# First query loads in 2 KB rows, landing times of a trace in the planner, and the tail constant behind unit eight

## The chip, the cores and the metric

The kernel runs on one core of a Trainium2 chip. The core has five engines that take instructions in order: TensorE (PE in the profile; its weight loads stand apart as PEld), VectorE (DVE), ScalarE (ACT), GpSimd (POOL) and SyncE (SP, which only issues DMAs here). Transfers run on 16 DMA engines. The metric is the device time of one execution in microseconds.

## The reference

Two stages. The first is a causal retention over 8 batches of 8 heads, 576 positions and 64 dimensions; the second is a two-layer network with a squared ReLU over all 4608 tokens.

```python
scores = scale * np.matmul(q, k.transpose(0, 1, 3, 2))
gamma = 1.0 - 2.0 ** (-5.0 - np.arange(H, dtype=np.float32))
Dmat = np.where(rel >= 0, gamma[:, None, None] ** rel[None, :, :], 0.0)
x = np.matmul(scores * Dmat, v)          # heads side by side: 4608 x 512
h = x @ w_in                             # 512 x 2048
out = np.maximum(h, 0.0) ** 2 @ w_out    # 2048 x 512
```

## The kernel before

**Units and groups.** A unit is 128 positions of one batch with all heads; there are 36, of which four are "tails" made of the last 64 positions of two batches. Two units form a group, so there are 18 groups. Each group passes through retention (scores, mask, state, output, xT) and then through the network: `ph` = w_in times xT (L876), ReLU (L884) and square (L894 or L896) into gT, and the product with w_out into `po`. Group 0 does that last product directly (L916). Every later group does it by Strassen's scheme with seven half-size products (L973): it needs sums of gT blocks (gS, L946, four a group on DVE) and differences of w_out blocks (wT, L827, four in all, on DVE).

**The first eight units are loaded in pairs.** `add_load_pair` brings 256 positions in one DMA of 512 KB; a partition holds two neighbouring positions, so a row is 512 bytes (L316). `add_unit_pair` casts the two halves to fp16 on DVE, ACT or POOL (kx, qx; L424), scales v (vx, L420), transposes k and q on PE into PSUM (psT, L439) and copies them out (kqT, L450). `add_ret_pair` does the rest: scores psc in two halves e, masked with `mask2` (rx, L490), state sums psS, the state R (L461, L514), outputs psO and xT (L577). Later units load q in four DMAs with 1 KB rows (L298), cast on POOL and are transposed by DMA (L400).

**What sets the order.** No order is written by hand: every step is a task of the class `Schedule` with an engine, a key (lower goes first), a planned duration and dependencies. `emit` runs an event loop over these planned times and writes the instructions in the order in which the tasks started. On the chip every engine then runs its list in that order and waits at each instruction for its own data. So a planned duration changes no work, only the order. DMA landings are planned as tasks of the engine SP: a duration, then `after` until the data count as there, with corrections in `LAG`.

**Start.** SP issues k0, q0, v0, k2, q2, v2 in this order (`FIRST`; 0 and 2 are pairs), then POOL issues the eight weight loads w0 to w7 with a cast to fp16 (L331; w0 to w3 are w_in, w4 to w7 are w_out), the first of them not before v0 has landed. k4 waits on SP until w5 has landed. PE has `WARM` matmuls without use (tile warm, L256) with the lowest priority, which fill its list where nothing else was ready in the plan.

**The tail constant.** `make_tail_pool` (L272, L273) makes iota_pt on POOL; then DVE makes vdl_tail (L182) and ACT vdec_tail (L184), which the v of a tail unit needs. `add_gated` enters it under ("v", 4); such a gate is read only in `add_unit`, which makes it wait for that unit's v cast. Unit 4 goes through `add_unit_pair`.

Of the kernel before, what the change touches and what calls it, by code (L numbers as in the profile page):

```python
# [15 lines left out]
class Schedule:  # L16
# [7 lines left out]
    def add(self, eng, key, dur, fn, deps=(), acq=(), after=None, lag=0.0):  # L24
        t = dict(eng=eng, key=key, dur=dur, fn=fn, acq=acq, n=len(self.tasks), users=[], free=[], lag=lag,
                 left=len(deps), ready=0.0, lat=self.LAT[eng] if after is None else after)
        for d in deps:
            d["users"].append(t)
        self.tasks.append(t)
        return t  # L30
# [11 lines left out]
    def emit(self):  # L42
        ready = {e: [] for e in self.LAT}
        busy = {e: False for e in self.LAT}
        events = []
        order = []
        seq = 0

        def push(at, what, t):
            nonlocal seq  # L50
            seq += 1
            heapq.heappush(events, (at, seq, what, t))
        for t in self.tasks:
            if t["left"] == 0:
                heapq.heappush(ready[t["eng"]], (t["key"], t["n"], t))
        now = 0.0
        while True:
            for e in ready:
                if busy[e]:
                    continue  # L60
                held = []
                while ready[e]:
                    item = heapq.heappop(ready[e])
                    t = item[2]
                    if all(self.count[r] >= t["acq"].count(r) for r in t["acq"]):
                        for r in t["acq"]:
                            self.count[r] -= 1
                        t["start"] = now
                        order.append(t)
                        busy[e] = True  # L70
                        push(now + t["dur"], "end", t)
                        break
                    held.append(item)
                for item in held:
                    heapq.heappush(ready[e], item)
            if not events:
                break
            now = events[0][0]
            while events and events[0][0] <= now + 1e-9:
                _, _, what, t = heapq.heappop(events)  # L80
                if what == "end":
                    busy[t["eng"]] = False
                    for w in t["users"]:

                        push(now + (0.0 if w["eng"] == t["eng"] else t["lat"]), "dep", w)
                    for g in t["free"]:
                        push(now + t["lat"], "free", g)
                elif what == "dep":
                    t["left"] -= 1
                    if t["left"] == 0:  # L90
                        push(now + t["lag"], "go", t)
                elif what == "go":
                    heapq.heappush(ready[t["eng"]], (t["key"], t["n"], t))
                else:
                    t["left"] -= 1
                    if t["left"] == 0:
                        self.count[t["res"]] += 1
        assert len(order) == len(self.tasks)
        for t in order:
            t["fn"]()  # L100
# [3 lines left out]
def kernel(  # L104
# [106 lines left out]
    mask2 = const.tile([P, 2, 2, 64], FP32, name="mask2")  # L211
    nc.gpsimd.memset(mask2, 1.0)
    for c in range(2):
        for e in range(2):
            m = mask2[c * 64:(c + 1) * 64, e]
            nc.gpsimd.affine_select(out=m, in_=m, compare_op=ALU.is_ge, fill=0.0, base=-e, pattern=[[1, 2], [2, 64]],  # L216
                                    channel_multiplier=-2)
# [7 lines left out]
    WARM = 34  # L225
# [4 lines left out]
    BESIDE = 1.1  # L230
# [6 lines left out]
    LAG = {"k4": 0.7, "q4": 0.5}  # L237
# [37 lines left out]
    tail_pool = add_gated("POOL", 4, "v", 2.2, make_tail_pool)  # L275
# [32 lines left out]
    def add_load_pair(name, u):  # L308
        n = "kqv".index(name)

        def fn():
            if name != "q":
                tile_of["stage", u] = stage.tile([P, 2, H, 2 * D], FP32, name="pair", tag="wst")
            x = tile_of[name + "32", u] = tile_of["stage", u][:, n % 2]
            b, c = units[u][1:]
            t = nc.sync.dma_start(out=x, in_=(k, q, v)[n][b, :, c * P:(c + 2) * P, :].rearrange("h (p e) d -> p h (e d)", e=2))  # L316
            if (name, u) == ("k", 4):
                behind(t, tile_of["w", 5])
            tile_of["load", name, u] = t
        loaded[name, u] = loaded[name, u + 1] = dma_task(0, 1.81 if loaded else 2.9, fn, acq=("wst",) if name != "q" else (),  # L320
# [4 lines left out]
    def add_weight(i):  # L325
# [10 lines left out]
        t = add("SP", 0, 2.75, lambda: None, deps=last_load + [issue], after=2.1 + LAG.get(f"w{i}", 0.0))  # L336
# [25 lines left out]
    def half(x):  # L362
        return slice(64 * x, 64 * x + 64)
# [39 lines left out]
    def add_unit_pair(u, base):  # L403
# [4 lines left out]
        for i, name in enumerate("kqv"):  # L408
            xs[name] = []
            for e in range(2):  # L410
                eng = ("DVE" if (e if name == "v" else lead) else "ACT" if name == "k" and u >= 4 or u == 2 and e else
                       "DVE" if name == "q" and u == 2 else "POOL")

                def fc(name=name, e=e, eng=eng):
# [4 lines left out]
                    if name == "v":  # L419
                        (nc.vector if eng == "DVE" else nc.gpsimd).tensor_tensor(  # L420
                            out=t.rearrange("p (h d) -> p h d", d=D), in0=x,
                            in1=vdec[f"pair{e}"].rearrange("p (h o) -> p h o", o=1).to_broadcast([P, H, D]), op=ALU.mult)
                    else:
# [10 lines left out]
        for i, name in enumerate("kq"):  # L434
# [9 lines left out]
            for s in range(2):  # L444
                on_act = i == 0 or s == 0 or u > 0

                def fe(i=i, s=s, on_act=on_act):
                    if i == 0:
                        tile_of["kqT", u + s] = work.tile([P, 2 * NP, P], FP16, name="kqT", tag="kqT", bufs=6)
                    (nc.scalar.copy if on_act else nc.vector.tensor_copy)(  # L450
                        out=tile_of["kqT", u + s][:, i * NP:(i + 1) * NP].rearrange("p x (e t) -> p e x t", e=2),
                        in_=tile_of["psT", u, i][:, :, :, half(s)])
# [15 lines left out]
    def add_ret_pair(g):  # L468
# [7 lines left out]
        for e in range(2):  # L476
# [11 lines left out]
            for a in range(2):  # L488
                def fm(e=e, a=a):
                    nc.vector.tensor_tensor(  # L490
                        out=rT[e][:, a], in0=rT["ps", e][a].rearrange("p (n i) -> p n i", i=P),
                        in1=mask2[:, e].rearrange("p (o e) i -> p o (e i)", o=1).to_broadcast([P, NP, P]), op=ALU.mult)
# [80 lines left out]
        for s in range(2):  # L573
            def fx(s=s):
                if s == 0:
                    tile_of["x", g] = x_pool.tile([P, NP, 2 * P], FP16, name="xT", tag="xT")
                nc.vector.tensor_tensor(  # L577
                    out=tile_of["x", g][:, :, s * P:(s + 1) * P].rearrange("p n (i e) -> p n e i", e=2),
                    in0=tile_of["psO", g][s].rearrange("p (n e i) -> p n e i", n=NP, e=2),
                    in1=gam_f.rearrange("p n (i e) -> p n e i", e=2), op=ALU.mult)  # L580
# [120 lines left out]
    def after_sums(g, t, key, res):  # L701
# [24 lines left out]
        r2 = add("DVE", key + 0.3, 0.65, fr2, deps=[r1], acq=("R",))  # L726
# [95 lines left out]
    def add_wT(i, in0, in1):  # L822
        ts = []
        for h in range(2):
# [3 lines left out]
            ts.append(add("DVE", WT_KEY + i, 0.7, f, deps=sum((wcast[j] for j in range(4, 8 if i else 6)), [])))  # L828
# [6 lines left out]
    for x, y in ((t2, t1), (t4, t2)):  # L835
        for p in y:
            for w in x:
                sched.need(w, p)
# [19 lines left out]
    def add_ff(g):  # L858
# [10 lines left out]
        for fb in range(NF // nf):  # L869
# [18 lines left out]
            def fg(fb=fb, on_act=on_act):  # L888
# [6 lines left out]
                else:  # L895
                    nc.vector.tensor_tensor(out=t, in0=rl, in1=rl, op=ALU.mult)  # L896
            r = add("ACT", place(4 * fb + 4), 0.6, fr, deps=[f1[-1]], acq=("rl",))
            sched.free("ff", [r])
            sq.append(add("ACT" if on_act else "DVE", place(4 * fb + 6), 0.63 if on_act else 0.55, fg, deps=[r] + sq[:1],
                          acq=() if fb else ("g",)))  # L900
# [31 lines left out]
    def add_strassen(g, us, base, sq):  # L932
# [7 lines left out]
        def add_sum(k, key, parts, in0, in1, op, deps, start=()):  # L940
            out_ = []
            for h in range(parts):
# [4 lines left out]
                out_.append(add("DVE", key + h, (BESIDE if h else 0.5) if parts > 1 else 0.8, f, deps=deps(h, parts) + list(start)))  # L947
# [164 lines left out]
```

## Time and profile before

| | us |
|---|---|
| median of 8 runs (lowest, highest) | 289.8 (289.52, 290.01) |
| the profiled execution | 289.78 |
| its span, first to last instruction | 288.1 |
| busy: DVE, ACT, POOL | 176.2, 187.4, 85.8 |
| xT of the first group done on DVE | 16.0 |
| first `ph` matmul | 17.73 |
| last matmul ends | 283.96 |
| k0, v0 landed (issue at 0.81 and 1.95; 4.2 and 6.7 us to landing) | 5.0, 8.7 |
| w0, w1 landed (issue at 8.96 and 11.01; 8.4 and 8.8 us to landing) | 17.4, 19.8 |

The profiled execution took 1.68 us more than its span; that share lies before the first and after the last instruction. Times in the text are from the start of the span. The granted clock was 0.998 of full speed. In the profile a busy share is given in tenths for forty slices of the span, a group of instructions by its line in the code and the names of its tiles, and a wait by what released it.

### The profile page before, as it was taken

To read this page: it belongs to the slowest core of one execution; us is meant where nothing else is said; L and a number is where in the kernel's file an instruction comes from. 1 tells how busy PE (TensorE), PEld (TensorE's weight loads), DVE (VectorE), ACT (ScalarE), POOL (GpSimd) and SP (SyncE) were. 2 spreads that over 40 slices of the span, in tenths; PEclk is the share of its full clock that TensorE was granted. 3 is DMA by queue.
4 is the path that set the end of the run, shared out by engine and by line. 5 is a ranking of instruction groups with operands and counts; after the bars stand their busy time and mean duration, and the time that the engine had idled before them with its cause. 6 is when DMAs were issued, how large, how long until landed. Compare 5 with 4: busy or idle time off the path is not lost.

```text
span 288.1 us, 10135 instructions
## 1 busy us (share of the span) xinstructions
PE 281.4 (98%) x4346; PEld 236.4 (82%) x4346; DVE 176.2 (61%) x341; ACT 187.4 (65%) x363; POOL 85.8 (30%) x124
## 2 busy tenths in 40 slices
PE   7999999999999999999999999999999999999994
PEld 3568767888888888888888888888888888888883
DVE  3772389768666756647656575766575566364632
ACT  4558975667585857657576748575848675847830
POOL 5560045333514242433425151534324000000000
PEclk9999999999999999999999999999999999999999
DMA  7999999999999898999789998979889420102004
GB/s 200 276 208 206 247 288 275 180 240 157 237 189 164 211 196 222 173 212 173 202 163 215 219 186 190 203 196 243 182 176 222 106 77 2 73 2 75 0 4 144
DMA packets 122156, 49.94 MB, mean 173 GB/s; under 512 B 94720, under 2 KB 117760, under 8 KB 122112
## 3 DMA queue, kind: packets, MB, share of 16 engines
q1 hardware_dynamic: 117568, 44.84, 70.3%
q0 software_dynamic: 4224, 4.19, 8.8%
q8 instruction: 34, 0.56, 0.9%
q10 hardware_dynamic: 320, 0.26, 0.4%
q14 instruction: 10, 0.08, 0.1%
HBM read 36.70 MB, written 9.44 MB: 160 GB/s over the span
## 4 chain that ended last, share of the span: by engine, by line
PE 91%; DMA 3%; POOL 2%; issue 2%; DVE 0%; POOLq 0%; DVEq 0%
PE ph L876 44%; PE po L973 37%; PE psO L357 4%; DMA w_in<-in_moe_w_in_dram 3%; PE po L916 2%; PE psc L357 2%; PE psS L357 2%; PE psT L439 1%; POOL mask L216 0%; POOL vx L420 0%; POOL w_in L331 0%; DVE o L996 0%; POOL mask_full L208 0%; POOL mask_tail L208 0%; DVE p L1025 0%
## 5 line engine op out<-in xcount | busy, mean ns | idle before, releaser
L876 PE MATMUL ph<-xT,w_in 128*128 128x256 f16 x1152 | 136.6, 273 | 0.2 <-DMA w_in<-in_moe_w_in_dram 0.2
L876 PEld LDWEIGHTS <-w_in 128*128 128x128 f16 x1152 | 111.3, 98 | 14.7 <-DMA w_in<-in_moe_w_in_dram 0.5
L884 ACT ACTIVATE rl<-ph 128x512 f16<-128x512 f32 x144 | 84.3, 586 | 50.6 <-PE ph L876 48.0
L894 ACT ACTIVATE gT<-rl 128x512 f16<-128x512 f16 x118 | 74.4, 631 | 3.4
L973 PEld LDWEIGHTS <-gS 128*128 128x128 f16 x544 | 51.7, 98 | 6.5
L973 PE MATMUL po<-wT,gS 128*128 128x256 f16 x408 | 55.8, 273 | 0.0
L946 DVE TENSOR_TENSOR gS<-gT,gS 128x512 f16<-128x512 f16 (+1 forms) x51 | 30.7, 601 | 23.9 <-ACT gT L894 23.3
L973 PEld LDWEIGHTS <-gT 128*128 128x128 f16 x408 | 39.6, 98 | 4.8
L973 PE MATMUL po<-w_out,gT 128*128 128x256 f16 x272 | 36.7, 273 | 0.0
L387 POOL TENSOR_TENSOR v<-v,vdec_full 128x512 f16<-128x512 f32 x24 | 26.6, 1106 | 26.3 <-DMA v<-in_v_dram 20.8
L946 DVE TENSOR_TENSOR gS<-gT 128x1024 f16<-128x1024 f16 x34 | 25.4, 747 | 7.0 <-ACT gT L894 6.9
L371 POOL CAST kq<-k 128x512 f16<-128x512 f32 x28 | 19.0, 677 | 34.5 <-DMA k<-in_k_dram 31.3
L382 POOL CAST kq<-q 128x512 f16<-128x512 f32 x24 | 15.1, 628 | 36.3 <-DMA q<-in_q_dram 36.2
L896 DVE TENSOR_TENSOR gT<-rl 128x512 f16<-128x512 f16 x26 | 12.2, 467 | 19.7 <-ACT rl L884 19.7
L996 DVE TENSOR_TENSOR o<-po,u 128x256 f32<-128x256 f32 x33 | 13.9, 421 | 15.5 <-PE po L973 7.9
L986 ACT COPY u<-po 128x256 f32<-128x256 f32 x34 | 12.5, 368 | 15.7 <-PE po L973 15.5
L751 DVE TENSOR_TENSOR xT<-psO,gam_full 128x512 f16<-128x512 f32 x28 | 18.0, 684 | 4.4 <-PE psO L357 4.0
L996 DVE TENSOR_TENSOR o<-po,p 128x256 f32<-128x256 f32 x18 | 7.6, 423 | 21.1 <-ACT u L986 13.1
L973 PE MATMUL po<-w_out,gS 128*128 128x256 f16 x136 | 18.0, 273 | 0.0
L973 PE MATMUL po<-wT,gT 128*128 128x256 f16 x136 | 17.6, 273 | 0.0
L692 DVE TENSOR_TENSOR rT<-psc,mask_full 128x512 f16<-128x512 f32 x24 | 15.6, 682 | 3.2 <-PE psc L357 3.0
L1047 ACT COPY o<-po 128x256 f32<-128x256 f32 x16 | 5.9, 370 | 10.4 <-PE po L973 8.8
(82 smaller groups left out, 226.6 us busy)
## 6 DMA issues: line engine op xcount, KB each, us to landing
out_dram<-o SPq DMA_DIRECT2D x32, 256.0 KB, 2.7
k<-in_k_dram SPq DMA_DIRECT2D x24, 256.0 KB, 4.5
q<-in_q_dram SPq DMA_DIRECT2D x96, 64.0 KB, 3.2
v<-in_v_dram SPq DMA_DIRECT2D x24, 256.0 KB, 3.8
pair<-in_k_dram SPq DMA_DIRECT2D x4, 512.0 KB, 7.0
pair<-in_q_dram SPq DMA_DIRECT2D x4, 512.0 KB, 7.0
pair<-in_v_dram SPq DMA_DIRECT2D x4, 512.0 KB, 7.0
w_in<-in_moe_w_in_dram POOLq DMA_DIRECT2D x4, 512.0 KB, 9.1
```

The source lines that it names most:

```text
L357: t = nc.tensor.matmul(out_, lhsT=lhsT, rhs=rhs, start=start, stop=True, skip_group_check=True, tile_position=(64 * row, 64 * col))
L371: op(out=out_.rearrange("p (n b a d) -> p n b a d", n=2, b=2, a=2), in_=in_.rearrange("p (a n b) d -> p n b a d", n=2, a=2))
L382: nc.gpsimd.tensor_copy(out=tile_of["kq", u][:, 1].rearrange("p (t a d) -> p a t d", t=4, a=2), in_=tile_of["q32", u].rearrange("p (a t) d ...
L387: nc.gpsimd.tensor_tensor(out=t, in0=tile_of["v32", u], in1=vdec[kind].rearrange("p (h o) -> p h o", o=1).to_broadcast([P, H, D]), op=ALU. ...
L692: tile_of["masking", g] = nc.vector.tensor_tensor(out=tile_of["rT", g][:, :, a], in0=tile_of["psc", g][a].rearrange("p (s n i) -> p s n i" ...
L751: nc.vector.tensor_tensor(out=tile_of["x", g].rearrange("p n (s e i) -> p e (n s) i", s=n, e=2)[:, c], in0=y.rearrange("p (o t r) -> p o r ...
L876: nc.tensor.matmul(tile_of["ph", g, fb][:, j, :], lhsT=w_in16[:, m, fi * P:(fi + 1) * P], rhs=tile_of["x", g][:, m, :], start=(m == 0), st ...
L884: nc.scalar.activation(out=t, in_=tile_of["ph", g, fb], func=ACTF.Relu)
L894: nc.scalar.activation(out=t, in_=rl, func=ACTF.Square)
L946: nc.vector.tensor_tensor(out=tile_of["S", g][:, k, sl], in0=in0(sl), in1=in1(sl), op=op)
L973: nc.tensor.matmul(tile_of["pb", g, bank], lhsT=left(i), rhs=right[:, i, :], start=(start and i == 0), stop=(i == HF - 1), skip_group_chec ...
L996: nc.vector.tensor_tensor(out=o_tile(u)[:, half * HM:(half + 1) * HM], in0=bank(x), in1=tile_of[name, g], op=ALU.add)
```

## The change

It has four parts.

1. A paired q is loaded by two DMAs of 256 KB, one for each half of the heads; a partition takes eight neighbouring positions of one head in each, a row of 2 KB. Which position lies in which partition and column thereby changes for q, and with it the cast of q, the copy of its transpose (kqT, both for q alone), `mask2` and the order in which xT is written.
2. The planner gets other numbers: planned durations and landings of the loads, a smaller `WARM`, and a model in which certain DVE tasks (`soft`) advance at 0.22 of their speed while a POOL task longer than 0.5 us runs. For group 1 the squares on DVE, the last ReLU and the sums get an earlier key (`HURRY`). A difference of w_out waits only for the weight loads that it reads.
3. All four casts of k and q for units 2 and 3 go to ACT (before: one each on POOL and DVE, two on ACT).
4. The tail constant is entered under ("v", 8), and unit 8 goes through `add_unit`.

```diff
@@ -21,8 +21,10 @@
-    def add(self, eng, key, dur, fn, deps=(), acq=(), after=None, lag=0.0):
-        t = dict(eng=eng, key=key, dur=dur, fn=fn, acq=acq, n=len(self.tasks), users=[], free=[], lag=lag,
+    SHARED = 0.22
+    def add(self, eng, key, dur, fn, deps=(), acq=(), after=None, lag=0.0, soft=False):
+        t = dict(soft=soft, eng=eng, key=key, dur=dur, fn=fn, acq=acq, n=len(self.tasks), users=[], free=[], lag=lag,
                  left=len(deps), ready=0.0, lat=self.LAT[eng] if after is None else after)
@@ -54,6 +56,17 @@
         now = 0.0
+        port = dict(task=None, left=0.0, at=0.0, beside=False)
+        def shared(beside):
+            t = port["task"]
+            if t is not None:
+                port["left"] -= (now - port["at"]) * (self.SHARED if port["beside"] else 1.0)
+                port["at"] = now
+                t["end"] = now + max(port["left"], 0.0) / (self.SHARED if beside else 1.0)
+                push(t["end"], "end", t)
+            port["beside"] = beside
         while True:
@@ -68,7 +81,14 @@
                         busy[e] = True
-                        push(now + t["dur"], "end", t)
+                        t["end"] = now + t["dur"]
+                        if t["soft"]:
+                            port.update(task=t, left=t["dur"], at=now)
+                            shared(port["beside"])
+                        else:
+                            push(t["end"], "end", t)
+                        if e == "POOL" and t["dur"] > 0.5:
+                            shared(True)
                         break
@@ -79,7 +99,14 @@
                 if what == "end":
+                    if abs(t["end"] - now) > 1e-6:
+                        continue
+                    t["end"] = -1.0
                     busy[t["eng"]] = False
+                    if t["soft"]:
+                        port["task"] = None
+                    elif t["eng"] == "POOL" and t["dur"] > 0.5:
+                        shared(False)
                     for w in t["users"]:
@@ -208,12 +235,12 @@
-    mask2 = const.tile([P, 2, 2, 64], FP32, name="mask2")
+    mask2 = const.tile([P, 2, 8, 16], FP32, name="mask2")
     nc.gpsimd.memset(mask2, 1.0)
             m = mask2[c * 64:(c + 1) * 64, e]
-            nc.gpsimd.affine_select(out=m, in_=m, compare_op=ALU.is_ge, fill=0.0, base=-e, pattern=[[1, 2], [2, 64]],
+            nc.gpsimd.affine_select(out=m, in_=m, compare_op=ALU.is_ge, fill=0.0, base=-e, pattern=[[1, 8], [8, 16]],
                                     channel_multiplier=-2)
@@ -222,19 +249,19 @@
     L = 2 * NF
-    WARM = 34
+    WARM = 26
     EARLY = 20
     QL = 0.8
-    BESIDE = 1.1
+    HURRY = 60
     PAUSE = 1.5
     JOIN = 5
-    LAG = {"k4": 0.7, "q4": 0.5}
+    LAG = {"k0": 0.3, "q0": 0.6, "v0": 0.3, "k2": 0.2, "q2": 0.5, "v2": 1.0, "w2": 0.7, "w7": 1.4, "k4": 0.3, "q4": 1.1, "v4": 0.9, "q6": 0.8, "v6": 0.2}
     LAG_T, LAG_O = 1.5, 5.0
@@ -272,7 +299,7 @@
-    tail_pool = add_gated("POOL", 4, "v", 2.2, make_tail_pool)
+    tail_pool = add_gated("POOL", 8, "v", 0.45, make_tail_pool)
     tail_dec = add("DVE", 0, 0.3, lambda: make_vdec("tail", tile_of["iota_pt"]), deps=[tail_pool])
@@ -313,11 +340,17 @@
             b, c = units[u][1:]
-            t = nc.sync.dma_start(out=x, in_=(k, q, v)[n][b, :, c * P:(c + 2) * P, :].rearrange("h (p e) d -> p h (e d)", e=2))
+            src = (k, q, v)[n][b, :, c * P:(c + 2) * P, :]
+            if name == "q":
+                for a in range(2):
+                    t = nc.sync.dma_start(out=x[:, NP * a:NP * a + NP].rearrange("p t d -> p (t d)"),
+                                          in_=src.rearrange("(a x) (r t) d -> a r x (t d)", a=2, t=8)[a])
+            else:
+                t = nc.sync.dma_start(out=x, in_=src.rearrange("h (p e) d -> p h (e d)", e=2))
             if (name, u) == ("k", 4):
             tile_of["load", name, u] = t
-        loaded[name, u] = loaded[name, u + 1] = dma_task(0, 1.81 if loaded else 2.9, fn, acq=("wst",) if name != "q" else (),
+        loaded[name, u] = loaded[name, u + 1] = dma_task(0, 2.9 if not loaded else 1.41 if name == "q" else 1.81, fn, acq=("wst",) if name != "q" else (),
                                                          after=2.1 + LAG.get(name + str(u), 0.0))
@@ -333,7 +366,7 @@
         issues.append(issue)
-        t = add("SP", 0, 2.75, lambda: None, deps=last_load + [issue], after=2.1 + LAG.get(f"w{i}", 0.0))
+        t = add("SP", 0, 2.58, lambda: None, deps=last_load + [issue], after=3.0 + LAG.get(f"w{i}", 0.0))
         last_load[:] = [t]
@@ -408,8 +441,7 @@
             for e in range(2):
-                eng = ("DVE" if (e if name == "v" else lead) else "ACT" if name == "k" and u >= 4 or u == 2 and e else
-                       "DVE" if name == "q" and u == 2 else "POOL")
+                eng = ("DVE" if (e if name == "v" else lead) else "ACT" if name == "k" and u >= 4 or u == 2 and name != "v" else "POOL")
@@ -420,6 +452,9 @@
                             in1=vdec[f"pair{e}"].rearrange("p (h o) -> p h o", o=1).to_broadcast([P, H, D]), op=ALU.mult)
+                    elif name == "q":
+                        x = tile_of["q32", u].rearrange("p (a t) (s d) -> p a (t s) d", a=2, s=2)[:, :, NP * e:NP * e + NP]
+                        engines[eng](out=t.rearrange("p (t a d) -> p a t d", t=NP, a=2), in_=x)
                     else:
@@ -447,9 +482,13 @@
                         tile_of["kqT", u + s] = work.tile([P, 2 * NP, P], FP16, name="kqT", tag="kqT", bufs=6)
-                    (nc.scalar.copy if on_act else nc.vector.tensor_copy)(
-                        out=tile_of["kqT", u + s][:, i * NP:(i + 1) * NP].rearrange("p x (e t) -> p e x t", e=2),
-                        in_=tile_of["psT", u, i][:, :, :, half(s)])
+                    out_, in_ = tile_of["kqT", u + s][:, i * NP:(i + 1) * NP], tile_of["psT", u, i]
+                    if i == 0:
+                        out_, in_ = out_.rearrange("p x (e t) -> p e x t", e=2), in_[:, :, :, half(s)]
+                    else:
+                        out_ = out_.rearrange("p x (t r) -> p t x r", r=16)
+                        in_ = in_.rearrange("p e y (r x) -> p (e y) x r", x=NP)[:, :, :, 16 * s:16 * s + 16]
+                    (nc.scalar.copy if on_act else nc.vector.tensor_copy)(out=out_, in_=in_)
                 es.append(add("ACT" if on_act else "DVE", base + 3 + i + s / 2, 0.66, fe, deps=[t] + T["kqT", u + s],
@@ -489,7 +528,7 @@
                         out=rT[e][:, a], in0=rT["ps", e][a].rearrange("p (n i) -> p n i", i=P),
-                        in1=mask2[:, e].rearrange("p (o e) i -> p o (e i)", o=1).to_broadcast([P, NP, P]), op=ALU.mult)
+                        in1=mask2[:, e].rearrange("p (o t) r -> p o (t r)", o=1).to_broadcast([P, NP, P]), op=ALU.mult)
                 ms.append(add("DVE", base + 5 + e, 0.66, fm, deps=[t] + ms))
@@ -575,9 +614,9 @@
                 nc.vector.tensor_tensor(
-                    out=tile_of["x", g][:, :, s * P:(s + 1) * P].rearrange("p n (i e) -> p n e i", e=2),
-                    in0=tile_of["psO", g][s].rearrange("p (n e i) -> p n e i", n=NP, e=2),
-                    in1=gam_f.rearrange("p n (i e) -> p n e i", e=2), op=ALU.mult)
+                    out=tile_of["x", g][:, :, s * P:(s + 1) * P].rearrange("p n (r t) -> p n r t", t=8),
+                    in0=tile_of["psO", g][s].rearrange("p (n t r) -> p n r t", n=NP, t=8),
+                    in1=gam_f.rearrange("p n (r t) -> p n r t", t=8), op=ALU.mult)
             T["x", u + s] = add("DVE", base + 25 + s, 0.7, fx, deps=[t] + ([T["x", u]] if s else []), acq=() if s else ("x",))
@@ -723,7 +762,7 @@
         r1 = add("DVE", key + 0.2 - URGENT, 0.69, fr1, deps=[r0])
-        r2 = add("DVE", key + 0.3, 0.65, fr2, deps=[r1], acq=("R",))
+        r2 = add("DVE", key + 0.3, 0.62, fr2, deps=[r1], acq=("R",), soft=True)
         T["Rm", g], T["R", g], T["Rread", g], T["Rmread", g] = r0, r2, [], r1
@@ -825,7 +864,7 @@
                 nc.vector.tensor_tensor(out=wT[i][:, sl], in0=in0[:, sl], in1=in1[:, sl], op=ALU.subtract)
-            ts.append(add("DVE", WT_KEY + i, 0.7, f, deps=sum((wcast[j] for j in range(4, 8 if i else 6)), [])))
+            ts.append(add("DVE", WT_KEY + i, 0.68, f, deps=wcast[4 + h] + (wcast[6 + h] if i else []), soft=True))
         return ts
@@ -833,9 +872,8 @@
     for x, y in ((t2, t1), (t4, t2)):
-        for p in y:
-            for w in x:
-                sched.need(w, p)
+        for w, p in zip(x, y):
+            sched.need(w, p)
     wT_done = {7: t3, 6: t2, 5: t1, 4: t4}
@@ -894,10 +932,10 @@
                     nc.vector.tensor_tensor(out=t, in0=rl, in1=rl, op=ALU.mult)
-            r = add("ACT", place(4 * fb + 4), 0.6, fr, deps=[f1[-1]], acq=("rl",))
+            r = add("ACT", place(4 * fb + 4) - HURRY * (g == 1 and fb == 7), 0.6, fr, deps=[f1[-1]], acq=("rl",))
             sched.free("ff", [r])
-            sq.append(add("ACT" if on_act else "DVE", place(4 * fb + 6), 0.63 if on_act else 0.55, fg, deps=[r] + sq[:1],
-                          acq=() if fb else ("g",)))
+            sq.append(add("ACT" if on_act else "DVE", place(4 * fb + 6) - HURRY * (g == 1 and not on_act), 0.63 if on_act else 0.43, fg, deps=[r] + sq[:1],
+                          acq=() if fb else ("g",), soft=not on_act))
             sched.free("rl", [sq[-1]])
@@ -944,7 +982,7 @@
                     nc.vector.tensor_tensor(out=tile_of["S", g][:, k, sl], in0=in0(sl), in1=in1(sl), op=op)
-                out_.append(add("DVE", key + h, (BESIDE if h else 0.5) if parts > 1 else 0.8, f, deps=deps(h, parts) + list(start)))
+                out_.append(add("DVE", key + h - HURRY * (g == 1), 0.43 if parts > 1 else 0.72, f, deps=deps(h, parts) + list(start), soft=True))
             sums[k] = out_
         nb = len(sq) // 2
```

## The prediction

> **What bounds the kernel now.** I read the stretches of the span first, with the busy time of each engine in each (columns: stretch, its length, busy us and instructions of PE, PEld, DVE, ACT, POOL, then clock, DMA share and GB/s), and beside it the same stretches for the useless tile warm.
>
> ```profile
> 0.00:17.00 17.00, 15.11 (x202) 7.58 (x202) 10.70 (x49) 8.58 (x19) 11.21 (x31) 1.00 1.02 233
> 17.00:20.00 3.00, 2.77 (x50) 2.15 (x50) 2.90 (x7) 1.15 (x3) 2.36 (x4) 1.00 1.24 206
> 20.00:52.00 32.00, 31.82 (x450) 24.19 (x449) 19.20 (x33) 24.45 (x47) 8.26 (x10) 1.00 1.15 249
> 52.00:283.00 231.00, 230.72 (x3641) 201.84 (x3640) 142.24 (x252) 153.25 (x296) 63.95 (x80) 1.00 0.74 160
> ```
> ```profile
> 0.00:17.00 17.00, 10.91 (x34) 1.00 1.02 233
> 17.00:20.00 3.00, 0.10 (x1) 1.00 1.24 206
> 20.00:52.00 32.00, 0.00 (x0) 1.00 1.15 249
> ```
>
> From 20 us on PE is idle for 0.18 + 0.28 us in all: nothing is to be won there. In the first 20 us it works 17.88 us, but 11.01 of these are warm matmuls, so only 6.87 us are of use. All that can be gained lies in the first 20 us, and what happens later can only lose. The timeline of PE shows what ends that phase (columns: start, length, instruction, idle time before and its releaser):
>
> ```profile
> 16.06 1.04 PE L256 MATMUL warm<-wT 128*128 128x512 f16 x4
> 17.03 0.77 PE L357 MATMUL psc<-kqT 64*64 64x128 f16 x32
> 17.73 1.92 PE L876 MATMUL ph<-xT,w_in 128*128 128x256 f16 x16
> 19.89 1.48 PE L876 MATMUL ph<-xT,w_in 128*128 128x256 f16 x12 [0.23 <-DMA w_in<-in_moe_w_in_dram]
> 21.30 0.64 PE L357 MATMUL psO<-rx,vx 64*64 64x128 f16 x32
> ```
>
> The last real wait is for w1 at 19.89. The chain of waits, cut to this stretch, leads there as well:
>
> ```profile
> 8.96 0.98 POOL w_in L331
> 9.95 0.07 issue
> 10.02 0.99 POOL vx L420
> 11.01 8.84 DMA w_in<-in_moe_w_in_dram
> 19.84 0.05 issue
> 19.89 1.48 PE ph L876 x12
> ```
>
> Its 8.84 us are not the cost of one transfer but a place in a queue. The DMA view of 2 to 13 us and of 13 to 33 us (packets, mean rate) shows that the engines never pause:
>
> ```profile
> DMA packets 6167, 3.12 MB, mean 284 GB/s; under 512 B 83, under 2 KB 6167, under 8 KB 6167
> ```
> ```profile
> DMA packets 4154, 4.15 MB, mean 207 GB/s; under 512 B 125, under 2 KB 4150, under 8 KB 4150
> ```
>
> First come the six paired loads in 512 B packets, then the weights, whose 207 GB/s written are 414 GB/s read, since the cast halves them. Each load delays all behind it. Issue plus time to landing gives k0 5.0, q0 6.8, v0 8.7, k2 10.5, v2 14.0, w0 17.4, w1 19.8, w2 22.4, w3 24.9 us: a paired load takes 1.8 us of the stream, a weight 2.5.
>
> [...] 1 KB rows of later q loads land 64 KB in 0.16 us (issues at 68.3 and 69.0 landed after 4.1 and 3.6 us, all four within 0.5 us), 1.3 us for 512 KB. [...] The kqT copy on DVE does 128x512 in 424 ns, faster than the 679 ns of a masked 128x512 from fp32 PSUM[...], and the new copy reads with a step of four. [...] gS of 128x1024 took 931 ns at 47.73, beside casts on POOL, against 688 elsewhere.
>
> **The change part by part.**
>
> *q in 2 KB rows.* The same 512 KB per pair in 256 packets instead of 1024. Bounds: 1.27 us at the 414 GB/s at which the weights' 2 KB rows are read[...]. I take 1.34, near the rate seen on this chip[...]: 0.47 us saved a load. q0 and q2 stand ahead of w1, so 2 x 0.47 = **0.94 us**[...]. The second issue costs SP some 0.43 us (the 1 KB-row issues at 69.0 and later). It hides: v0 is issued at 1.95, k2 at 3.36, seconds in the queue before their turn; without that cover v0 would be 0.43 later. w0's own issue waits for v0, which comes 0.47 earlier (q0 alone). Only 7 packets of its queue are seen before 13 us, while the paired packets run until 13.4; they would now end near 12.5 and w0's packets could start from 12.4, so no hole opens. q4 and q6 save 0.94 more behind the weights.
>
> *What is late next.* With w1 at 18.9, ph of w0 must be done by then: w0 at 16.4, 1.75 us of matmul, 18.2. It needs xT of group 0, at 16.0 now. That chain moves too: k0 landed at 5.0, but the timeline of DVE has its cast behind vdl_tail, which waited 2.55 us for iota_pt:
>
> ```profile
> 5.73 0.23 DVE L182 TENSOR_SCALAR vdl_tail<-lnrow,iota_pt 128x8 f32<-128x8 f32 x1 [2.55 <-POOL iota_pt L273]
> 5.86 0.76 DVE L424 CAST kx<-pair 128x512 f16<-128x512 f32 x2
> ```
>
> This wait goes (part 4) and gives some 0.7 us; q0 comes 0.47 earlier. Against it the strided DVE copy of q for unit 1 goes from 0.42 to at most 0.69 (+0.27). So xT falls near 15.5, before 16.4: all three are hidden by w0, and cost or give nothing. Without that cover the copy would cost its 0.27. The ACT copies (592 ns) may stay[...]; the trace has none like it. I take 0, since ACT has 1.6 of 4 us free in 12 to 16 us.
>
> *Casts of units 2 and 3.* POOL and DVE lose one of 0.62 and 0.42; ACT gains 2 x 0.62. q2's first cast now stands at 13.48 on DVE, behind the state updates, though q2 is there by about 12.3; on ACT it can go at landing. That takes a us or more off psc of group 1, now at 17.03 just behind the four warm ones. If rx and thus psO of group 1 (1.0 us of PE, now at 21.3, behind w1) come before w1's arrival, PE does up to 0.7 us of it in the gap that opens between 18.2 and 18.9. DVE is the limit: 3.82 and 3.68 of 4 us busy in 12 to 20, with rx ending at 20.0. I expect it to end near 18.7 and count **0.2 us** (0 to 0.7).
>
> *Planner.* 26 instead of 34 warm matmuls: eight of 0.216 are 1.7 us, about what the shorter start takes from the need for them; they never stood before anything that w1 doesn't gate. If too few, PE idles a us; [...] no idle gap in this trace after 1.3 us reaches even 0.3 us. `HURRY` brings four sums and the DVE squares of group 1 ahead of group 2's retention on DVE: of these only the 0.93 us at 47.73 stood behind rx of group 2. xT of group 2 is ready at 50.53 and its ph starts at 51.98, so 1.45 us are free, and group 2's loads come 0.94 to 1.4 earlier. Nothing.
>
> *Same cost.* The mask, xT and q's POOL casts keep sizes and counts; xT of the later units already reads with a step of 16 elements and takes 684 ns against 726 here. The tail constant later costs 0.18 + 0.22 on POOL, 0.23 on DVE and 0.30 on ACT, beside PE.
>
> Sum: 289.78 - 0.94 - 0.2 = **288.6 us**. This is against the profiled execution, 0.02 below the median of 289.8.
>
> **The rivals.** *A, the forecast:* w1 and all behind it move up. [...] *B, more:* psO of group 1 is wholly done before w1; for it, 2 us less on the cast path; against it, the full DVE. 289.78 - 0.94 - 1.0 = 287.8. *C, hidden anyway:* the order planned anew opens small gaps behind 20 us that eat most of it, say 0.04 us in each of 17 groups, 0.7: 289.5. For it, that PE has no gap to lose there and so every change of order is a risk; against it, that DVE has some 40% free. *D, slower:* vdl_tail now stands on DVE behind unit 8's v cast, and DVE waits there if that cast is planned too early, as it waited 2.55 us at the start. The cast ended at 50.97 in the trace, just where xT of group 2 (49.19 to 50.53), rx of group 3 and the sums are queued. If DVE reaches vdl_tail ahead of xT of group 2 and POOL is no earlier than now, then xT comes at 50.97 + 0.45 + 0.23 + 1.35 = 53.0, against a need at 51.98 - 1.14 = 50.84: 2.2 us lost, 1.0 net, 290.8. It decides against the change once that wait makes xT later than 52.6; v of unit 8 landing 1.9 us earlier (all four q) speaks against it. *E, that part 4 doesn't do what it says:* it does move the constant, since unit 4 never reads a gate; but the wait it ends was hidden by w0, so its worth is nothing and it lies inside A, without a chance of its own.
>
> **How the numbers follow.** A 0.60, B 0.10, C 0.14, D 0.16. About 0.2% is what a measurement of this kernel can tell from no change, so faster means below 289.2, slower above 290.4: A and B give 0.70 faster, C 0.14 the same, D 0.16 slower. From 287.8 to 289.7 lie A, C and most of B, some 0.8.
>
> **What would show it.** Right: w1's wait of PE ends near 18.9; paired q packets of 2 KB and 1.3 us between the landings of k and v less a k's own 1.8; vdl_tail after 45 us with no long wait; PE idle after 20 us still below 0.6. Wrong: w1 no earlier (the stream had a hole), a wait of DVE for iota_pt near 50, a PE gap before ph of group 2, or warm matmuls in front of ph.

## The result, and the profile after

The changed kernel takes 291.88 us (median of 11 runs, 290.5 to 293.22), the kernel before beside it on the same chip 289.83 us (31 runs, 289.52 to 290.99): a ratio of 1.0068, 95% interval 1.0055 to 1.0081. It is 2 us slower; 288.6 us had been predicted. Ratios and spreads in this text leave out four executions of the runs below that lay more than 1.5% above the fastest of their kernel; the medians count all. The profiled execution took 292.88 us with a span of 291.1, 3.0 more than before.

The stretches of the span, the first view shown of the kernel before, now of the changed one (columns as there):

```profile
0.00:17.00 17.00, 13.30 (x226) 7.26 (x226) 11.14 (x47) 9.11 (x20) 11.28 (x30) 1.00 0.99 244
17.00:20.00 3.00, 3.00 (x30) 2.63 (x31) 2.93 (x8) 1.75 (x4) 1.09 (x2) 1.00 1.24 206
20.00:52.00 32.00, 29.25 (x417) 21.99 (x415) 19.14 (x33) 23.87 (x46) 8.15 (x12) 1.00 1.08 239
52.00:283.00 231.00, 230.72 (x3638) 201.16 (x3638) 142.70 (x251) 153.31 (x296) 64.39 (x80) 0.99 0.75 158
```

Read the third line: from 20 to 52 us PE now works 29.25 of 32 us where it worked 31.82. One hole makes this up, as PE's timeline shows:

```profile
17.10 3.23 PE L914 MATMUL ph<-xT,w_in 128*128 128x256 f16 x28
20.27 0.64 PE L390 MATMUL psO<-rx,vx 64*64 64x128 f16 x32
51.98 0.60 PE L1011 MATMUL po<-w_out,gS 128*128 128x256 f16 x4 [2.58 <-ACT u L1024]
```

The first two lines are the good half: all 28 matmuls of ph run without a wait for w1, and psO of group 1 starts at 20.27 instead of 21.30. The third is the bad half: po waits 2.58 us for a copy u on ACT, which reads an earlier po out of PSUM. The chain of waits, cut to this place, says why u is late:

```profile
45.04 4.05 DMA v<-in_v_dram
49.09 0.07 issue
49.16 1.04 POOL v L420
50.20 0.13 POOL iota_pt L299
...
50.42 0.23 POOL iota_pt L300
...
50.68 0.68 DVE vdl_tail L209
...
51.38 0.30 ACT vdec_tail L211
51.67 0.27 ACT u L1024
51.94 0.04 issue
51.98 0.60 PE po L1011 x4
```

This is the whole tail constant, from v of unit eight on: cast, iota_pt, vdl_tail, vdec_tail, and only then u. u needs none of it; it merely stands behind vdec_tail on its engine. How long the two engines stood is in the brackets of their timelines:

```profile
50.68 0.67 DVE L209 TENSOR_SCALAR vdl_tail<-lnrow,iota_pt 128x8 f32<-128x8 f32 x1 [2.87 <-POOL iota_pt L300]
51.38 0.30 ACT L211 ACTIVATE vdec_tail<-vdl_tail,lnscale 128x8 f32<-128x8 f32 x1 [5.20 <-DVE vdl_tail L209]
```

Behind the hole the clock falls. The stretch 53.3 to 56.8 us (the granted clock stands third from the end):

```profile
53.30:56.80 3.50, 3.50 (x19) 2.51 (x17) 2.60 (x7) 0.37 (x1) 0.98 (x1) 0.51 1.03 218
```

At 0.51 of full speed some 1.7 us of work are lost in it (3.5 x 0.49). The account of this execution: 289.78 - 1.03 (psO earlier) + 2.58 (hole) + 1.7 (clock) = 293.0, against 292.88.

It holds for this execution and not for each. Every execution has its mean granted clock on record, and 3.4 us at half speed take 0.006 from it. Of the twelve of this kernel seven show 0.994 or less, five 0.997 or more. These five, which have no room for such a stretch, are no faster: 291.87 us in the median, against 292.02. What they lose in its place no trace shows.

### The profile page after: what moved, and what is told of

Read it like the earlier page. It is cut to its first block, busy times and chain, and to the rows that moved or that the text cites. A ratio compares the mean times of both kernels' runs of the same rounds, so it can differ in the third digit from the quotient of the medians.

```text
span 291.1 us, 10125 instructions
## 1 busy us (share of the span) xinstructions
PE 280.2 (96%) x4338; PEld 236.4 (81%) x4338; DVE 177.9 (61%) x340; ACT 188.4 (65%) x365; POOL 84.9 (29%) x123
## 4 chain that ended last, share of the span: by engine, by line
PE 89%; DMA 3%; DVE 3%; ACT 1%; issue 1%; SPq 1%; POOL 0%; DVEq 0%
PE ph L914 43%; PE po L1011 36%; PE psO L390 4%; PE po L954 2%; PE psc L390 2%; DMA pair<-in_v_dram 2%; PE psS L390 2%; DMA v<-in_v_dram 1%; DVE rx L529 1%; DVE R L500 1%; PE psT L474 0%; DVE vx L452 0%; SPq L346 0%; ACT gT L932 0%; ACT rl L922 0%
## 5 line engine op out<-in xcount | busy, mean ns | idle before, releaser
L1011 PEld LDWEIGHTS <-gT 128*128 128x128 f16 x408 | 40.2, 99 | 5.2
L984 DVE TENSOR_TENSOR gS<-gT,gS 128x512 f16<-128x512 f16 (+1 forms) x51 | 30.0, 589 | 22.2 <-ACT gT L932 21.7
L984 DVE TENSOR_TENSOR gS<-gT 128x1024 f16<-128x1024 f16 x34 | 26.0, 765 | 6.4 <-ACT gT L932 6.3
L415 POOL CAST kq<-q 128x512 f16<-128x512 f32 x24 | 15.5, 646 | 38.3 <-DMA q<-in_q_dram 38.1
L1034 DVE TENSOR_TENSOR o<-po,u 128x256 f32<-128x256 f32 x33 | 13.9, 421 | 16.4 <-PE po L1011 8.0
L1011 PE MATMUL po<-wT,gT 128*128 128x256 f16 x136 | 18.5, 281 | 0.0
L500 DVE TENSOR_TENSOR R<-stmp,dec 128x512 f16<-128x512 f32 (+1 forms) x18 | 12.9, 717 | 0.5
```

The costliest lines, as they stand in the source:

```text
L500: nc.vector.tensor_tensor(out=out_.rearrange(shape, s=n, n=NP), in0=in_.rearrange(shape, s=n, n=NP), in1=dec128.rearrange("p (s n o) -> p ...
L984: nc.vector.tensor_tensor(out=tile_of["S", g][:, k, sl], in0=in0(sl), in1=in1(sl), op=op)
L1011: nc.tensor.matmul(tile_of["pb", g, bank], lhsT=left(i), rhs=right[:, i, :], start=(start and i == 0), stop=(i == HF - 1), skip_group_chec ...
L1034: nc.vector.tensor_tensor(out=o_tile(u)[:, half * HM:(half + 1) * HM], in0=bank(x), in1=tile_of[name, g], op=ALU.add)
```

## The experiments

The theory at the start: the tail constant holds DVE and ACT, and that is the whole loss. Rivals: the rows do less than thought, or the other planner numbers cost something. Every run beside the kernel before; ratios are to it.

**Both tail instructions later** (the changed kernel; POOL's part stays behind unit eight):

```
-    tail_dec = add("DVE", 0, 0.3, lambda: make_vdec("tail", tile_of["iota_pt"]), deps=[tail_pool])
+    tail_dec = add("DVE", 0, 0.3, lambda: 0, deps=[tail_pool])
...
+            if u == 12:
+                make_vdec("tail", tile_of["iota_pt"])
```

> The changed kernel with vdl_tail and vdec_tail written out later, ahead of the v cast of unit 12; the order of all other instructions on every engine is the same, and iota_pt stays where it is. Theory 1 (the wait for the tail constant makes the PE gap of 2.58 us and the slower clock after it): no PE gap above 0.3 us near 50 us, no half clock near 53 us, 288.4 to 288.9 us. Theory 2 (group 3 is late by the new order, and the wait only shows where it is late): a gap of 1.5 us or more stays, 290.3 us or more.

**Only the instruction on ACT later** (vdl_tail keeps its place on DVE, the Exp goes ahead of unit 12's v cast):

> The changed kernel with only vdec_tail, the ACT half of the constant, written out later (ahead of the v cast of unit 12); vdl_tail still waits on DVE for iota_pt. If the hold on ACT, where copies of u and ReLUs stand behind vdec_tail, is what stops PE: within 0.5 us of the run with both later, though DVE still waits some 2.9 us. If the hold on DVE, where rx of group 3 stands behind vdl_tail, is what stops it: within 0.7 us of the changed kernel, 291 us or more.

They took 290.64 us (1.0020, 1.0002 to 1.0037) and 290.73 us (1.0028, 1.0015 to 1.0042). In the second, DVE still waited 1.9 us for iota_pt, and PE had no hole at po: u ran at 48.88 us as soon as its po was done.

```profile
  POOL iota_pt L309: 1.9, 1
```
```profile
48.88 0.37 ACT L1035 COPY u<-po 128x256 f32<-128x256 f32 x1 [2.54 <-PE po L1022]
```

So it is ACT's queue that made the hole, not DVE's. DVE's is not free, though. In the same execution PE stood just behind that place for rx, which follows vdl_tail on DVE; with both instructions later it did not:

```profile
50.78 0.41 PE L399 MATMUL psc<-kqT 64*64 64x128 f16 x15 [0.46 <-DVE rx L540]
```

The hole is gone in both runs, and yet the time is only 1.2 us lower, still above before, and not the 288.4 to 288.9 expected. Some of it can be seen: the half clock was not in every execution of the changed kernel, and in the profile of the first run here another one stands at the start (told below). The rest says that the theory can't be the whole.

**The tail constant alone, in the kernel before:**

```
-    tail_pool = add_gated("POOL", 4, "v", 2.2, make_tail_pool)
+    tail_pool = add_gated("POOL", 8, "v", 0.45, make_tail_pool)
```

> The kernel before with the tail constant alone entered behind unit 8; PE, and the rest of DVE, ACT and POOL, keep their order. Theory 1: DVE and ACT wait here too, until POOL has cast v of unit 8 (ended at 50.97 us in the trace of before), and PE loses 0.5 to 3 us: 290.3 to 293. Theory 2 (it needs the new order): within 0.6 us of before.

289.92 us, 0.9997 (0.9984 to 1.0009): it costs nothing there. In that order vdl_tail comes at 53.1 us, after iota_pt, and no engine waits for it.

**The rows alone, in the kernel before** (the q loads, and the layouts that they bring; planner, casts and tail constant as before):

```
+            if name == "q":
+                for a in range(2):
+                    t = nc.sync.dma_start(out=x[:, NP * a:NP * a + NP].rearrange("p t d -> p (t d)"),
+                                          in_=src.rearrange("(a x) (r t) d -> a r x (t d)", a=2, t=8)[a])
```

> The kernel before with the paired q in two DMAs of 2 KB rows and what follows from it (cast, copy of the transpose, mask, xT), with the planner's numbers and every engine's order as before. By the sum on record: w1 lands 0.9 us earlier and the time falls to 288.8 to 289.2. If the new planner numbers made the start shorter, not the rows: within 0.3 us of before.

289.81 us, 1.0006 (0.9986 to 1.0025): no gain. w1 landed at 19.47 instead of 19.84 and nobody waited for it, yet psO of group 1 started when it had before:

```profile
18.13 3.23 PE L889 MATMUL ph<-xT,w_in 128*128 128x256 f16 x28
21.29 0.64 PE L363 MATMUL psO<-rx,vx 64*64 64x128 f16 x32
```

What is late next is the attention chain in front of ph (18.13 against 17.73). One link of it grew: the cast of q for unit 2 on DVE, in the kernel before and with the rows alone:

```profile
13.48 0.42 DVE L424 CAST qx<-pair 128x512 f16<-128x512 f32 x1
```
```profile
13.90 1.27 DVE L431 CAST qx<-pair 128x512 f16<-128x512 f32 x1
```

The new layout alone doesn't do that: the two casts of q for units 0 and 1 took 0.76 us together in both. Here POOL's vx ran beside the cast, from 13.69 to 14.89; before it started behind it, at 14.19. Part 3 of the change puts this cast on ACT. So the head start comes only with the new order and casts. Over all profiled runs psO of group 1 starts at 21.08 to 21.30 us in before's order and at 20.27 to 20.57 in the changed one with 26 warms, one run apart, which is told of below.

**The gate alone undone, in the changed kernel**, and three edits on top of it: the landing of kq's transposes counted at 6.0 us after the issue in the plan, instead of 3.0 (psc of the later groups moves back by 2 to 3 us); 34 warm matmuls; both.

```
-    tail_pool = add_gated("POOL", 8, "v", 0.45, make_tail_pool)
+    tail_pool = add_gated("POOL", 4, "v", 2.2, make_tail_pool)
...
-        T["kqT", u] = [add("SP", -1, 2.4, fx2, deps=[ck, cq], acq=("kqT",), after=3.0, lag=LAG_T)]
+        T["kqT", u] = [add("SP", -1, 2.4, fx2, deps=[ck, cq], acq=("kqT",), after=6.0, lag=LAG_T)]
...
-    WARM = 26
+    WARM = 34
```

What suggested the second: with the hole gone, PE waited in the middle of the kernel. PE in the kernel before, and in the run with only ACT's instruction later:

```profile
124.64 0.43 PE L357 MATMUL psc<-kqT 64*64 64x64 f16 x32
```
```profile
122.33 0.32 PE L399 MATMUL psc<-kqT 64*64 64x64 f16 x16 [1.01 <-DMA kqT<-kq]
```

The transpose that it waits for was issued at 117.97 us in the kernel before and at 118.53 in the other: SP's stream is no earlier at all there. Only psc has moved forward, from 124.64 to 121.3. The plan explains it. It gives a weight 2.58 us of SP's stream instead of 2.75, and each of four paired q loads 1.41 instead of 1.81; the later transposes of kq therefore stand 3.0 us earlier in it (8 x 0.17 + 4 x 0.40). The real stream of weights ended 1.0 us earlier (34.44 against 35.5 for w7), and by 118 us even that was gone in this run.

> The changed kernel with one edit: the tail constant's POOL part is tied to unit four's v again (estimate 2.2 us) instead of unit eight's. Theory (vector and scalar queues held by vdl_tail and vdec_tail were the whole fall): no TensorE gap of 2.58 us near 50 us and no half clock after it, time about that of the two runs that put the two instructions later, 290.6 to 290.8 us, that is 0.1 to 0.3% above the kernel before. Rival (the place of the tail constant costs little and the planner's other numbers hold the loss): 291.5 us or more.

> The run with the gate undone, and in the plan the landing of the DMA transposes of kq counted at 6.0 us after the issue instead of 3.0, so that the plan puts psc of every later group some 2 to 3 us further back. Theory (the head start is given back near 122 us because the plan, whose w loads and q loads became 3.0 us shorter in sum while the real stream moved by 1.0 us, puts psc of units 16 and 17 before their transpose has landed): no wait of psc for kqT at 122 us, 0.5 to 1.0 us gained on the run with the gate undone, time 289.7 to 290.2. Rival (the transposes are not what limits, or something else is late next): unchanged within 0.3 us.

> The run with the gate undone and 34 warm matmuls instead of 26, the order of the four other engines unchanged. Theory (too few warm matmuls leave TensorE partly idle in the first 17 us, and in part of the executions the granted clock falls to a half for 3.4 us there): spread of the runs narrower, median lower by 0.3 to 0.8 us than with 26. Rival (the eight warms only fill idle time that costs nothing): unchanged within 0.3 us; if they stand in front of ph or psc: slower by up to 1 us.

> Gate undone, transposes counted at 6.0 us in the plan and 34 warm matmuls. Theory: the two losses add up, time 288.8 to 289.5 us, faster than the kernel before (289.8) by 0.1 to 0.3%. Rival (the shorter start is always given back to the stream of transfers): 289.8 us or more.

The gate undone gave 291.19 us (1.0031, 1.0014 to 1.0049): not below the first two, but with a spread of 288.57 to 292.27. Its profiled execution was the fastest of them, a span of 286.9 us. There the transpose was issued at 116.21, no psc waited, and after 20 us nothing was lost:

```profile
20.00:52.00 32.00, 31.82 (x453) 24.21 (x451) 21.57 (x39) 25.41 (x48) 7.94 (x10) 1.00 1.17 244
52.00:280.00 228.00, 227.72 (x3616) 199.14 (x3614) 143.78 (x247) 152.00 (x293) 65.22 (x80) 1.00 0.76 160
```

So the forecast's 288.6 can be had; here the transfers came early and nothing waited for them. Most executions don't get it. Transposes counted at 6.0 us gave 290.24 us (1.0013, 1.0001 to 1.0025). 34 warms gave 291.05 (1.0037, 1.0021 to 1.0053): no gain from the filling as such. Both together gave 290.0 (0.9992, 0.9979 to 1.0005). The last two differ in the counted landing of the transposes alone; they lie 1 us apart, and their intervals don't meet. PE with 34 warms, then with the later psc too:

```profile
96.29 0.32 PE L390 MATMUL psc<-kqT 64*64 64x64 f16 x16 [0.55 <-DMA kqT<-kq]
...
122.69 0.32 PE L390 MATMUL psc<-kqT 64*64 64x64 f16 x16 [0.79 <-DMA kqT<-kq]
```
```profile
124.01 0.43 PE L390 MATMUL psc<-kqT 64*64 64x64 f16 x32
```

Both waits are gone. The hoped-for 288.8 to 289.5 was missed, though.

**Three controls.** The later psc in the changed kernel, with its gate and its 26 warms; an earlier psc in the kernel before (`after=0.0` for 3.0); and, on the run with 34 warms, the plan's stream made 2.0 us later in place of the transposes, so that it moves by 1.0 us against before's as the real one did:

```
-        t = add("SP", 0, 2.58, lambda: None, deps=last_load + [issue], after=3.0 + LAG.get(f"w{i}", 0.0))
+        late = 2.0 if i == 7 else 0.0
+        t = add("SP", 0, 2.58 + late, lambda: None, deps=last_load + [issue], after=3.0 - late + LAG.get(f"w{i}", 0.0))
```

> The changed kernel, tail constant still behind unit eight and 26 warm matmuls, with only the transposes of kq counted at 6.0 us in the plan (psc further back). Theory (the tail wait costs its full gap of about 2.6 us, and in the changed kernel it hides the early psc, since a TensorE that is 3 us late finds every transpose landed): the gap near 50 us stays, and the time stays within 0.5 us of the changed kernel's 291.9, that is 291.4 to 292.2. Rival (the early psc costs about 1 us in the changed kernel too): 290.6 to 291.2.

> The kernel before, with the transposes of kq counted at 0 us instead of 3.0 in its plan, which puts psc of the later groups about 3 us further forward, as the changed kernel's plan does; no other edit. Theory (the lost slack of psc is a cost of its own, whatever the rows, casts and tail constant): waits of psc for kqT of 0.5 us or more between 90 and 170 us, time 290.3 to 291.3, and a wider spread than before's. Rival (the slack isn't what the changed kernel lost): within 0.3 us of 289.8.

> Gate undone, 34 warm matmuls, and in the plan the end of the stream of w loads 2.0 us later with the landing of w7 unchanged, so that the plan's stream moves by 1.0 us against before's as the trace's did, not by 3.0; transposes at 3.0 us as in the changed kernel. Theory (the plan's loads and transposes ran 2 to 3 us ahead of the chip): about the same as the run with transposes at 6.0 us and 34 warms, 289.5 to 290.1, better than 34 warms alone by 0.8 us or more. Rival (only the place of psc by itself matters, or the new order of the stream loses elsewhere): 290.6 or more.

The first: 291.8 us (1.0073, 1.0044 to 1.0103), as without the edit. The hole is there again and the fall of the clock behind it, with a mean of 0.69 from 52.0 to 53.3 us and of 0.63 behind that. Its PE timeline and the second stretch:

```profile
51.82 0.60 PE L1011 MATMUL po<-w_out,gS 128*128 128x256 f16 x4 [2.06 <-ACT u L1024]
```
```profile
53.30:56.80 3.50, 3.50 (x22) 2.66 (x21) 2.10 (x5) 0.46 (x2) 1.05 (x2) 0.63 1.11 219
```

In the changed kernel the early psc costs nothing that these seven executions would show, and its own profile has no wait of psc behind the hole: a PE that is 3 us late found every transpose landed. The hole hides the second fault, and this is one reason why taking the hole away gave back so little.

The second: 291.48 us (1.0089, 1.0051 to 1.0127), somewhat more than the 290.3 to 291.3 expected. Four of the seven executions lie at 291.0 to 291.5, three at 294.0 to 294.4 with a mean granted clock of 0.991 to 0.992; the latter were not profiled. Neither rows nor casts nor the tail constant are changed in it, and PE waits at psc:

```profile
83.35 0.32 PE L357 MATMUL psc<-kqT 64*64 64x64 f16 x16 [0.54 <-DMA kqT<-kq]
...
109.86 0.32 PE L357 MATMUL psc<-kqT 64*64 64x64 f16 x16 [0.62 <-DMA kqT<-kq]
```

The slack of psc is thus worth more than 1 us by itself. The third: 289.28 us (18 runs, 288.61 to 292.64; ratio 0.9980, 0.9961 to 1.0000), a little below the 289.5 to 290.1 expected. By the two ratios it is some 1.7 us below the same kernel with the plan as it was (1.0037), with intervals that don't meet. It is the only run whose interval doesn't reach above 1; that it beats the kernel before is likely and not shown. One wait of psc is left in its profile:

```profile
96.58 0.32 PE L391 MATMUL psc<-kqT 64*64 64x64 f16 x16 [0.37 <-DMA kqT<-kq]
```

## Why the prediction was wrong

*The step that failed* is "The tail constant later costs ... beside PE", and with it rival D's condition. The sum took 0.30 us of ACT as work and not as a wait, and D looked at DVE alone: vdl_tail ahead of xT of group 2. In the trace xT of group 2 was done at 47.47 us and DVE reached vdl_tail after it, so D's condition was not met; yet PE stopped, because vdec_tail stood on ACT in front of u. Its 0.30 us of work held ACT for 5.20 us and PE for 2.58. The plan can't see that: the constant is one task of 0.3 us on DVE, and its instruction on ACT has no task. D had the place and the sign, with 290.8 us, but neither the queue nor the clock. What was to speak against D, v of unit eight 1.9 us earlier, didn't come: its cast started at 49.16 instead of 49.93, 0.8 earlier.

*"Planner ... Nothing"* failed too. Shorter loads in the plan are not only a tidier start: they moved psc of all later groups forward by some 3 us, with transfers that didn't follow. Rival C had small gaps behind 20 us at 0.7 in all; they come as one or two waits of psc of 0.4 to 1.0 us, and the pairs of runs that differ in psc's place put them at 1 us and more in the median. This fault is hidden in the changed kernel, which is why C would not have explained its time. By the ratios the gate is worth 1.1 us of the 2.0 (1.0068 against 1.0031), and the rest went only when psc got its slack back with 34 warms (0.9992 and 0.9980).

*The 0.94 of the rows* came in part, and on the wrong limit. In the changed kernel v0 landed at 8.30 us instead of 8.66 and v2 at 13.16 instead of 14.02, so the two q loads saved 0.36 and 0.50, together 0.86 us. The forecast was 0.47 each, with 0.54 as the most that the 414 GB/s of the weights allowed. From 5 to 13 us the transfers ran at 307 GB/s, where they ran at 290 before. With the rows alone v0 landed at 8.76 and v2 at 13.53: nothing saved on the first and 0.59 on the second. So half a us for the second load is seen twice, and the first is open. w1 landed 1.15 us earlier in the changed kernel and 0.37 with the rows alone, where the time didn't change. The wait of 0.23 us for w1 was the last one, but the attention chain was close behind it.

*That chain hidden by w0* is the other half of this. The forecast had xT of group 0 at 15.5 and w0 at 16.4, with the strided copy covered. w0 landed at 16.63 and ph started only at 17.10, behind psS and psc of group 1 (with 0.79 us of PE for which the profile names no releaser), so it is not w0 that starts ph now. The copy took 0.68 us for 0.42, as forecast (0.69 was the author's estimate, beside the 679 ns of a masked 128x512), but PE waited 0.45 us for it. A link that the sum left alone grew more: an update of the state R took 1.21 us for 0.42, again with POOL's vx beside it (13.32 to 14.36). So xT was done at 16.44, later than the 16.0 before:

```profile
13.43 1.21 DVE L500 TENSOR_TENSOR R<-stmp,dec 128x256 f16<-128x256 f32 x1
```

*The head start as a whole* was of the right size, and that is luck as much as insight: 1.14 predicted; psO of group 1 came 1.03 us earlier in the changed kernel, and the execution without a wait behind it ended 1.2 us under before's. But it came from a ph that started 0.63 earlier and then ran through, not from a later gap in front of w1. *The casts on ACT* took 1.5 us off psc of group 1, as forecast (15.52 for 17.03, all but three of its matmuls), but the 0.2 us that they were to give did not come that way: rx of group 1 ended at 19.62 and not near 18.7, and psO stands behind all of ph as before.

*The clock* was not in the sum. It fell after holes of 2.58 and 2.06 us (0.51 and 0.63 from 53.3 to 56.8), and once at the start, in the run with both instructions later. The eight warms less took 2.45 us from PE's work and not 1.7; with 26 PE has four holes of 0.38 to 0.66 us between 9 and 17 us in that run, and the stretch behind them shows the clock at 0.66:

```profile
17.00:22.00 5.00, 5.00 (x39) 3.63 (x40) 3.46 (x8) 2.89 (x5) 1.20 (x2) 0.66 1.24 208
```

There psO of group 1 began at 21.89, and the head start was lost. It is one of six profiles with 26 warms. The other five have three or four such holes, up to 0.99 us long, and no slow clock behind them, so what decides is not shown. None of the three with 34 in the changed order shows it. The mean clocks of all executions agree: without the hole at po, 22 of 72 with 26 warms are at 0.994 or less, one of 51 with 34. Still, 34 warms put psO at 20.63 to 21.04, some 0.4 later, and gained nothing in the median.

*Open:* only one execution of each kernel is profiled, so what makes the transfers late in one and early in the next (288.57 to 292.27 us for one kernel) was not seen; nor is it known what makes the clock fall in one and not in the next, how much slack psc needs, or whether the rest of the head start can be kept.

## What to carry to other kernels

An instruction that waits for late data holds everything behind it on its queue (here ACT for 5.20 us, and through u PE for 2.58), so a moved helper has to be followed on every engine that it issues to, and each needs a place in the plan. A forecast of transfer times that is a little short moves the consumers of all later transfers forward, and where the transfers don't follow, slack turns into waits (here of psc, 0.4 to 1.0 us each). When removing a large wait gives little back, look for the one that it hid: make it appear alone in the old kernel.

## What the hardware showed unasked

The granted clock went to one half for 3.4 us (53.35 to 56.76) after PE had been idle for 2.58 us, and began to do so 1.4 us after PE was at work again:

| stretch, us | granted clock |
|---|---|
| 53.2 to 53.3 | 1.00 |
| 53.3 to 53.4 | 0.75 |
| 53.6 to 55.0 | 0.50 |
| 55.0 to 56.5 | 0.50 |
| 56.7 to 56.8 | 0.69 |
| 56.8 to 56.9 | 1.00 |

In the other run with the hole 2.06 us of idle time came before it. If it fell to one half there as well, its means of 0.69 (52.0 to 53.3) and 0.63 (53.3 to 56.8) give an estimated 3.4 us that began 0.7 us after PE was at work again. At the start of the run with both instructions later, 0.66 from 17 to 22 us gives 3.4 us too, and PE had never rested longer than 0.66 us between 2 and 17 us. So the length comes out the same three times, and the idle time ahead of it differs.

ACT kept to the order of its list: vdec_tail waited 5.20 us, and u behind it, whose po ended at 48.53, came only at 51.67.
